# Weighing steps, output weights, gates and staged loads in a two-part attention kernel

## The chip, the cores and the metric

The kernel runs on one core of one Trainium2 chip. The metric is the time that the device needs for one execution, in microseconds (us); the kernel before is given by the median of three runs. The span in a profile is the time from the first to the last recorded event of one further execution, which the profiler recorded; that execution's own time is given beside its span.

The engines of the core are named as the profile names them: PE (TensorE, matrix products; PEld its weight loads), DVE (VectorE), ACT (ScalarE), POOL (GpSimd) and SP (SyncE, which here only issues DMAs). SPq and ACTq are DMA issues by SP and ACT.

## The reference

Two independent attentions over 2048 positions with model width 576 and 32 heads of width 18. Each ends in its own output projection, and the two outputs are put side by side. All of it is float32.

```
# A: one key head and one value head shared by 32 query heads, no mask
q = (x @ wq) in 32 heads;  k = x @ wk;  v = x @ wv          # k, v: 2048 x 18
p = softmax(q @ k.T * 18**-0.5)
outA = (p @ v) @ wo

# B: 32 heads, 4 segments of 512 positions, a memory M, z carried over the segments
phi = lambda t: where(t > 0, t + 1, exp(t))
g = sigmoid(beta)                                            # one number per head
M, z = 0, 0
for s in range(4):
    p = softmax(qs @ ks.T * 18**-0.5 + causal_mask)          # inside the segment
    a_dot = p @ vs
    a_mem = (phi(qs) @ M) / (phi(qs) @ z + 1e-6)
    o[s] = g * a_mem + (1 - g) * a_dot
    M, z = M + phi(ks).T @ vs, z + sum(phi(ks))
outB = o @ wo
```

## The kernel before

**First phase, 0 to about 330 us.** The projections of A and B are computed, each as a sum of products of split parts, and stored to DRAM scratch: `qA`, `kA`, `qB`, `kB`, `vB`. In the first 21 us the weights of A come in five pieces. ScalarE casts each to `wAh` (L196), VectorE takes the rest to `wAl` (L197), and TensorE begins to project (L208). In program order the gates come behind the first of A's four chunks of positions: `gt` becomes the sigmoid of beta, and `omg` is 1 minus it. Both are 128 x 5 tiles; column t holds the values of head tile t, one row per head and head dimension. The five loads of a column each (L267) are issued on ScalarE's DMA queue, with `gt`'s exponential (L270) on ScalarE and three small instructions on VectorE behind them. Further on, the memory's numerators `numB` (with the factor g in them) and denominators `denB` of segments 1 to 3 are computed and stored to scratch.

**Second phase, about 330 us to the end.** Attention runs in *turns*. A turn takes three score items. One item is two heads by 512 queries by 128 keys of A, or by one of three groups of keys of a segment of B. TensorE computes the scores into `E` (L765 for A, L774 for B). ScalarE exponentiates (L783), for one item of three from a copy `W` that VectorE made (L780). One of the 32 items of a block of A is exponentiated on VectorE by a polynomial instead (L738 to L748, with the tiles `PD` and `q`), one step a turn. For B, GpSimd then sets the masked half of the diagonal squares of `P` to zero (`affine_select`, L788). Two turns later TensorE multiplies `P` with the values into `O` (L813). VectorE copies `O` out, and SP stores it to scratch, `oA` or `oB` (L825). Row 0 of each head there is the sum of the softmax.

A *block* is four heads of one chunk (A) or of one segment (B): 32 blocks of A with 11 turns each, and 32 blocks of B with 2 turns each. The blocks of B are put in pairs behind blocks of A by the list `after`. Below, "segment 1, first pair" is the pair of blocks of B with heads 0 to 7 of segment 1. Every pair of blocks needs a stack of queries and keys (`stA`, `stB`), which `prefetch` loads ahead of its use, and every segment of B its values `vseg`.

**From the sums to the output projection.** The heads of a chunk or segment make five *head tiles*: t = 0 to 3 with 7 heads (126 rows), t = 4 with 4 heads (72 rows). Once the block with heads 24 to 27 is done (t = 0 to 3 follow from it), and again once the last block is done (t = 4), `finish` enters a chain of steps in a list `later`; `due` runs from it, once a turn, what has come up to its turn:

1. `begin`, one turn later: `sums` loads the softmax sums, and for segments 1 to 3 the denominators, into `sm`.
2. `inv`, `d1` turns later: `inverses` takes the reciprocal on VectorE (L618) and stores it to `rA`, `rB` and `rdB` in scratch (L620, L622).
3. `load`, as room is found: `load_heads` loads the head tile `o` (L632), the inverses spread over the rows, `rb` (L633), and for segments 1 to 3 also `numB` and the inverse denominators `rb2`.
4. `heads`, `d2` turns later: one GpSimd instruction per step, at most two in a turn. `weigh` gives them: for A the product with `rb` (L644); for B first the product with `omg` (L647, `part`), then that with `rb`; for segments 1 to 3 also the product of `nb` with `rb2`, and the addition.
5. When all five tiles are weighed, the output projection of that chunk or segment, `out_proj`, goes into `fill` one turn later. `run_fill` runs one step of four matrix products (L662) in a turn, 60 steps in all. It uses the weights `woA` and `woB`, which `load_wo` loads (L595) by five DMAs each.

What is left in `fill` after the last turn is run out, and then comes the projection of A's last chunk.

**What sets the order.** The instructions of PE, ACT and DVE are issued in the order written (`manual_schedule`). GpSimd's and SP's queues are not in that list: the scheduler orders them when the kernel is built, so a step that the program asks for in a later turn may stand earlier in those two queues.

Of the kernel before, what the change touches and what calls it, by code (L numbers as in the profile page):

```python
# [68 lines left out]
def attention_pair_kernel(ctx, tc, a_xT, a_w, a_wo, b_xT, b_w, b_wo, b_beta, ident_d, hmask_d, bmask_d, cmask_d, sel_d, zmask_d, selx_d, sely_d, out):  # L69
# [30 lines left out]
    gt = cp.tile([128, 5], F32, name="gt")  # L100
    omg = cp.tile([128, 5], F32, name="omg")
# [43 lines left out]
    with ExitStack() as ph:  # L145
# [75 lines left out]
        for c in range(NCH):  # L221
# [34 lines left out]
            if c == 0:  # L256
# [8 lines left out]
                for t in range(5):  # L265
                    lo, nh = H0[t], HT[t]
                    nc.scalar.dma_start(  # L267
                        gt[: RT[t], t : t + 1], b_beta[lo : lo + nh][:, None].to_broadcast([nh, DH])[:, :, None]
                    )
# [345 lines left out]
    def inverses(ab, c, lo, hi, said):  # L615
        sm, R, w, mem = said
        n = 2 if mem else 1
        nc.vector.reciprocal(sm[:R, :n], sm[:R, :n])  # L618
        r_d = rA if ab == "A" else rB
# [4 lines left out]
    def load_heads(ab, c, t):  # L624
        o_d, r_d = (oA, rA) if ab == "A" else (oB, rB)
        if (ab, c) not in parts:
            parts[ab, c] = pa.tile([128, 5, C], F32, name="o", bufs=2)
        tiles = [parts[ab, c][:, t], pa.tile([128, C], F32, name="rb", bufs=4)]
        if ab == "B" and c > 0:
            tiles += [pa.tile([128, C], F32, name=n, bufs=3) for n in ("nb", "rb2")]  # L630
        lo, n, R = H0[t], HT[t], RT[t]
        nc.sync.dma_start(tiles[0][:R], o_d[c][lo : lo + n, 1:VW, :])  # L632
        nc.sync.dma_start(tiles[1][:R], r_d[c][lo : lo + n, None, :].to_broadcast([n, DH, C]))  # L633
        if ab == "B" and c > 0:
            nc.sync.dma_start(tiles[2][:R], numB[c][DH * lo : DH * lo + R])
            nc.sync.dma_start(tiles[3][:R], rdB[c][lo : lo + n, None, :].to_broadcast([n, DH, C]))
        return tiles

    def weigh(ab, c, t, tiles):

        R = RT[t]
        o, rb = (x[:R] for x in tiles[:2])
        v = nc.gpsimd
        own = lambda: v.tensor_tensor(o, o, rb, op=ALU.mult)  # L644
        if ab == "A":
            return [own]
        part = lambda: v.tensor_scalar(o, o, omg[:R, t : t + 1], None, op0=ALU.mult)  # L647
        if len(tiles) == 2:
            return [part, own]
        nb, rb2 = (x[:R] for x in tiles[2:])  # L650
        return [
            part,
            own,
            lambda: v.tensor_tensor(nb, nb, rb2, op=ALU.mult),
            lambda: v.tensor_tensor(o, o, nb, op=ALU.add),
        ]
# [193 lines left out]

    def at(k, cost, ready, step):
# [3 lines left out]
    def due(k, most=2, heavy=2):  # L855

        cost = 0
        for e in [e for e in later if e[0] <= k]:
# [7 lines left out]
    def finish(k, ab, c, hg):  # L866
# [3 lines left out]
        box = {}  # L870
# [19 lines left out]
        def load(k, t):  # L890
            loaded[0] += 1
            box[t, t] = load_heads(ab, c, t)
            at(k + d2, 1, lambda: True, lambda k, t=t: heads(k, t))

        def heads(k, t):
            if not isinstance(box[t, t][0], type(heads)):
                box[t, t] = weigh(ab, c, t, box[t, t])
# [4 lines left out]
            loaded[0] -= 1  # L902
# [13 lines left out]
    with tc.manual_schedule(engines={ENG.PE, ENG.Activation, ENG.DVE}):  # L916
# [3 lines left out]
        turns, prods = [], []  # L920
# [6 lines left out]
        for k in range(len(turns) + 2):  # L927
# [108 lines left out]
```

## Time and profile before

| | before |
|---|---|
| median of 3 runs | 1471.53 us (1470.94 to 1474.15) |
| profiled execution, own time | 1476.41 us |
| its span | 1474.7 us |
| mean granted TensorE clock | 0.988 of full |
| ACT busy | 1194.1 us, 81% |
| DVE busy | 1030.4 us, 70% |
| POOL busy | 258.3 us, 18% |
| GpSimd masks (L788) | 192 instructions, 94.2 us |
| GpSimd products and sums of `weigh` (L644) | 40 instructions, 58.3 us |
| HBM traffic | 111 GB/s on average |

How to read the profile's lines: a row of the timeline has the start in us, the duration, the engine, the line, the operation, output<-inputs by the program's names, and the shapes; "x3" says how many neighbours were put together, and the brackets how long the engine had been idle before, and on what it waited. A row of a table of windows has the stretch, then the engine's busy time in it (with the number of instructions) for each engine asked for, the granted TensorE clock, the busy share of the DMA engines, and the DMA rate in GB/s. A row of waits has the waiting line and its releaser, the time in all, the number of waits, and the longest.

### The profile page before, as it was taken

To read this page: it belongs to the slowest core of one execution; us is meant where nothing else is said; L and a number is where in the kernel's file an instruction comes from. 1 tells how busy PE (TensorE), PEld (TensorE's weight loads), DVE (VectorE), ACT (ScalarE), POOL (GpSimd) and SP (SyncE) were. 2 spreads that over 40 slices of the span, in tenths; PEclk is the share of its full clock that TensorE was granted. 3 is DMA by queue.
4 is the path that set the end of the run, shared out by engine and by line. 5 is a ranking of instruction groups with operands and counts; after the bars stand their busy time and mean duration, and the time that the engine had idled before them with its cause. 6 is when DMAs were issued, how large, how long until landed. Compare 5 with 4: busy or idle time off the path is not lost.

```text
span 1474.7 us, 40733 instructions
## 1 busy us (share of the span) xinstructions
PE 1435.0 (97%) x17540; PEld 844.3 (57%) x17540; DVE 1030.4 (70%) x1209; ACT 1194.1 (81%) x1424; POOL 258.3 (18%) x311
## 2 busy tenths in 40 slices
PE   8889999999998999999999999999999999999998
PEld 5658878764454455555555555555555555555555
DVE  6474754646775577787777797777778887787761
ACT  3343334339998899999999999999999999999960
POOL 1031000001134112712110270031113500010001
PEclk9999999999999999999999999999999999999999
DMA  6775643445456154534222342233113221110022
GB/s 194 233 235 186 194 155 110 157 153 166 130 147 186 50 162 143 155 105 131 84 71 56 121 152 63 79 110 106 44 37 103 85 72 32 56 55 17 9 87 79
DMA packets 87986, 166.31 MB, mean 113 GB/s; under 512 B 12480, under 2 KB 21242, under 8 KB 87626
## 3 DMA queue, kind: packets, MB, share of 16 engines
q1 hardware_dynamic: 81510, 157.82, 34.2%
q10 hardware_dynamic: 6291, 5.85, 1.3%
q8 instruction: 138, 2.26, 0.6%
q14 instruction: 47, 0.38, 0.1%
HBM read 96.15 MB, written 67.49 MB: 111 GB/s over the span
## 4 chain that ended last, share of the span: by engine, by line
PE 60%; ACT 10%; issue 3%; DMA 2%; DVE 1%; SPq 1%; POOL 0%; ACTq 0%; DVEq 0%; POOLq 0%
PE O L813 28%; PE E L765 17%; PE F L662 11%; ACT P L783 10%; PE E L774 3%; PE E L662 1%; DMA oB<-oe 1%; DVE W L780 1%; PE O L662 1%; DMA rb<-rB 1%; DMA sm<-oA 0%; DMA rB<-sm 0%; SPq L595 0%; POOL o L644 0%; DVE q L742 0%
## 5 line engine op out<-in xcount | busy, mean ns | idle before, releaser
L783 ACT ACTIVATE P<-E 128x1024 f32<-128x1024 f32 (+1 forms) x800 | 788.4, 1077 | 23.2 <-PE E L765 11.4
L780 DVE COPY W<-E 128x1024 f32<-128x1024 f32 (+1 forms) x384 | 460.9, 1200 | 196.4 <-PE E L765 127.5
L813 PE MATMUL O<-P,VA 128*32 128x256 f32 x7936 | 511.4, 381 | 0.0
L783 ACT ACTIVATE P<-W 128x1024 f32<-128x1024 f32 (+1 forms) x384 | 433.9, 1130 | 2.0 <-DVE W L780 1.2
L813 PEld LDWEIGHTS O<-P,VA 128*32 128x32 f32 x7936 | 263.0, 110 | 148.1 <-issue 11.8
L765 PE MATMUL E<-stA,kstA 56*128 56x512 f32 x1920 | 331.4, 440 | 3.1 <-ACT P L783 1.5
L765 PEld LDWEIGHTS E<-stA,kstA 56*128 56x128 f32 x1920 | 155.0, 184 | 182.0 <-ACT P L783 121.3
L788 POOL TENSOR_SCALAR_AFFINE_SELECT P<-P 128x256 f32<-128x256 f32 (+1 forms) x192 | 94.2, 493 | 461.4 <-ACT P L783 427.5
L662 PE MATMUL F<-woB,o 126*32 126x192 f32 (+1 forms) x1920 | 127.8, 339 | 3.0 <-POOL o L644 3.0
L745 DVE SCALAR_TENSOR_TENSOR q<-q,PD 128x1024 f32<-128x1024 f32 x96 | 122.1, 1272 | 0.0
L644 POOL TENSOR_TENSOR o<-o,rb 126x512 f32<-126x512 f32 (+1 forms) x40 | 58.3, 1460 | 322.6 <-DMA o<-oA 143.2
L813 PE MATMUL O<-P,vseg 128*32 128x256 f32 (+2 forms) x1536 | 83.9, 349 | 4.0 <-POOL P L788 4.0
L110 ACT CAST qp<-pj 126x512 fp32r<-126x512 f32 (+1 forms) x56 | 32.6, 584 | 66.1 <-DVE kmB L360 49.8
L662 PEld LDWEIGHTS F<-woB,o 126*32 126x32 f32 (+1 forms) x1920 | 38.5, 108 | 72.7 <-issue 58.4
L662 PE MATMUL F<-woA,o 126*32 126x192 f32 (+1 forms) x1240 | 77.6, 338 | 1.7 <-DVE osb L687 1.7
L111 DVE TENSOR_TENSOR qp<-pj,qp 126x512 fp32r<-126x512 f32 (+1 forms) x56 | 38.3, 686 | 55.6 <-ACT qp L110 55.4
L208 PE MATMUL pj<-xh,wBh 128*126 128x512 f32 x180 | 73.7, 413 | 2.8 <-DVE xh L180 2.8
L822 DVE COPY oe<-O 128x512 f32<-128x512 f32 x64 | 44.3, 692 | 42.0 <-PE O L813 41.4
L208 PE MATMUL pj<-xh,wBl 128*126 128x512 f32 x180 | 72.2, 401 | 0.0
L813 PEld LDWEIGHTS O<-P,vseg 128*32 128x32 f32 x1536 | 48.4, 110 | 31.0 <-POOL P L788 5.5
L774 PE MATMUL E<-stB 56*128 56x256 f32 (+3 forms) x512 | 63.1, 354 | 2.4 <-ACT P L783 1.9
L208 PE MATMUL pj<-xl,wBh 128*126 128x512 f32 x144 | 59.8, 415 | 0.0
(134 smaller groups left out, 1400.1 us busy)
## 6 DMA issues: line engine op xcount, KB each, us to landing
stB<-kB SPq DMA_DIRECT2D x96, 144.0 KB
stB<-qB SPq DMA_DIRECT2D x32, 288.0 KB
stA<-qA SPq DMA_DIRECT2D x30, 288.0 KB
oA<-oe SPq DMA_DIRECT2D x32, 256.0 KB
oB<-oe SPq DMA_DIRECT2D x32, 256.0 KB
qA<-qp SPq DMA_DIRECT2D x16, 504.0 KB
kB<-qp SPq DMA_DIRECT2D x16, 504.0 KB
qB<-qp SPq DMA_DIRECT2D x16, 504.0 KB
```

Source lines behind the costliest of these rows:

```text
L111: nc.vector.tensor_tensor(qp[:R, 1, :n], src, qp[:R, 0, :n].bitcast(F32), op=ALU.subtract)
L208: nc.tensor.matmul(dst, w[:, c0 : c0 + M], x, start=i == 0, stop=i == len(ops) - 1)
L644: own = lambda: v.tensor_tensor(o, o, rb, op=ALU.mult)
L662: nc.tensor.matmul(dst[32 * j : 32 * j + 32], parts[ab, c][: RT[t], t, r0 : r0 + 32], wo[ab][: RT[t], t, c0 : c0 + n], start=start, stop=stop,
L745: steps.append(lambda a=a: v.scalar_tensor_tensor(q, q, a, p, op0=ALU.add, op1=ALU.mult))
L765: nc.tensor.matmul(e[:, j], kstA[rows, 128 * kt : 128 * kt + 128], st[rows, h, :], start=True, stop=True)
L774: nc.tensor.matmul(e[:, j, c0 : c0 + 512 - 128 * k], st[rows, 4 + h, ks], st[rows, h, 128 * k :], start=True, stop=True)
L780: nc.vector.tensor_copy(src[:, :, :n], e[:, :, :n])
L783: nc.scalar.activation(p[:, :, :n], src[:, :, :n], AF.Exp, scale=SCALE)
L788: nc.gpsimd.affine_select(diag, diag, pattern=[[0, 2], [0, m], [1, 128]], base=0, channel_multiplier=-1, compare_op=ALU.is_ge, fill=0.0)
L813: nc.tensor.matmul(o[32 * j : 32 * j + 32, q0 : q0 + n], v, p[:, j % 2, p0 : p0 + n], start=m == hf == 0, stop=last and hf == 1,)
L822: nc.vector.tensor_copy(osb, o)
```

## The change

- *Turns.* `due` lets no weighing step on GpSimd run in a turn when that turn or one of the two after it has score items of B (`near`).
- *Output weights.* `load_wo` is called in blocks 0 and 1 of A's first chunk, in place of blocks 2 and 5.
- *Gate.* `gt` and `omg` get two more columns, which hold the gate in the layout of the sums (4 rows a head for 28 heads; 32 rows a head for 4 heads), with two more loads on ScalarE's queue. `inverses` multiplies B's inverse sums by 1 - g on VectorE, and the `part` step (L647) is gone from `weigh`. All of `weigh` on GpSimd is then one instruction for A and for segment 0, and three for segments 1 to 3.
- *Stages.* `load` is split. `load_heads` loads `o` alone, right behind the inverses; `load_inverses` loads the rest `d2` turns later, when there is room in one pool of ten tiles, which takes the place of the pools of four, three and three. `heads` follows `d3` turns after that.
- *Delays.* Behind a block come: the sums after 2 turns (1 before), the inverses after 5 (4 or 5 before), the inverses' loads after 3 more, and the first weighing after 6 more (6 or 8 from the inverses before). For the last chunk: 0, 2, 0 and 3 (0, 2 and 3 before). `fill` gets the projection two turns after the last weighing (one before).

```diff
-    gt = cp.tile([128, 5], F32, name="gt")
-    omg = cp.tile([128, 5], F32, name="omg")
+    gt = cp.tile([128, 7], F32, name="gt")
+    omg = cp.tile([128, 7], F32, name="omg")
...
+                for t, lo, hi, n in ((5, 0, 28, 4), (6, 28, 32, 32)):
+                    nc.scalar.dma_start(
+                        gt[: n * (hi - lo), t : t + 1], b_beta[lo:hi][:, None].to_broadcast([hi - lo, n])[:, :, None]
+                    )
...
         nc.vector.reciprocal(sm[:R, :n], sm[:R, :n])
+        if ab == "B":
+            g = 5 if lo == 0 else 6
+            nc.vector.tensor_scalar(sm[:R, 0], sm[:R, 0], omg[:R, g : g + 1], None, op0=ALU.mult)
...
     def load_heads(ab, c, t):
...
+        nc.sync.dma_start(parts[ab, c][: RT[t], t], (oA if ab == "A" else oB)[c][H0[t] : H0[t] + HT[t], 1:VW, :])
+
+    def load_inverses(ab, c, t):
+        lo, n, R = H0[t], HT[t], RT[t]
+        tiles = [pa.tile([128, C], F32, name="rb", bufs=10)]
+        r_d = rA if ab == "A" else rB
+        nc.sync.dma_start(tiles[0][:R], r_d[c][lo : lo + n, None, :].to_broadcast([n, DH, C]))
         if ab == "B" and c > 0:
+            tiles += [pa.tile([128, C], F32, name="rb", bufs=10) for _ in range(2)]
+            nc.sync.dma_start(tiles[1][:R], numB[c][DH * lo : DH * lo + R])
+            nc.sync.dma_start(tiles[2][:R], rdB[c][lo : lo + n, None, :].to_broadcast([n, DH, C]))
         return tiles
...
-        own = lambda: v.tensor_tensor(o, o, rb, op=ALU.mult)
-        if ab == "A":
-            return [own]
-        part = lambda: v.tensor_scalar(o, o, omg[:R, t : t + 1], None, op0=ALU.mult)
-        if len(tiles) == 2:
-            return [part, own]
...
+        steps = [lambda: v.tensor_tensor(o, o, rb, op=ALU.mult)]
+        if mem:
+            nb, rb2 = mem
+            steps += [
+                lambda: v.tensor_tensor(nb, nb, rb2, op=ALU.mult),
+                lambda: v.tensor_tensor(o, o, nb, op=ALU.add),
+            ]
+        return steps
...
     def due(k, most=2, heavy=2):
         cost = 0
+        near = [its[n][0] for t in turns[k : k + 3] for n, pr in t]
+        heavy *= "B" not in near
...
-        d1, d2 = (2, 3) if last else (4, 6) if (ab, c) == ("B", 0) else (5, 8)
+        d0, d1, d2, d3 = (0, 2, 0, 3) if last else (2, 5, 3, 6)
...
             for t in ts:
-                at(k, 0, room, lambda k, t=t: load(k, t))
+                at(k, 0, place, lambda k, t=t: load(k, t))
+
+        def place():
+            return (ab, c) in parts or len(parts) - filled[0] // FILL < 2
+
+        def load(k, t):
+            load_heads(ab, c, t)
+            at(k + d2, 0, room, lambda k: weights(k, t))
...
         def room():
-            return loaded[0] < (3 if ab == "B" and c > 0 else 4) and ((ab, c) in parts or len(parts) - filled[0] // FILL < 2)
+            return loaded[0] + need <= 10
+
+        def weights(k, t):
+            loaded[0] += need
+            tiles = load_inverses(ab, c, t)
+            box[t, t] = weigh(ab, c, t, tiles)
+            at(k + d3, 1, lambda: True, lambda k: heads(k, t))
...
-                at(k + 1, 0, lambda: True, lambda k: fill.append(out_proj(ab, c)))
+                at(k + 2, 0, lambda: True, lambda k: fill.append(out_proj(ab, c)))
-        at(k + (0 if last else 1), 0, lambda: hg not in summing, begin)
+        at(k + d0, 0, lambda: hg not in summing, begin)
...
-                    if it in (("A", 0, 2, 4), ("A", 0, 5, 4)):
-                        load_wo(*(("B", b_wo) if it[2] == 2 else ("A", a_wo)))
+                    if it in (("A", 0, 0, 8), ("A", 0, 1, 8)):
+                        load_wo(*(("B", b_wo) if it[2] == 0 else ("A", a_wo)))
```

More of the change, by code (lines that the diff above doesn't have):

```diff
@@ L637, in load_heads @@
         return tiles
     def weigh(ab, c, t, tiles):
-        R = RT[t]
-        o, rb = (x[:R] for x in tiles[:2])
+        o, (rb, *mem) = parts[ab, c][: RT[t], t], [x[: RT[t]] for x in tiles]
         v = nc.gpsimd
-        own = lambda: v.tensor_tensor(o, o, rb, op=ALU.mult)
-        if ab == "A":
-            return [own]
-        part = lambda: v.tensor_scalar(o, o, omg[:R, t : t + 1], None, op0=ALU.mult)
-        if len(tiles) == 2:
-            return [part, own]
-        nb, rb2 = (x[:R] for x in tiles[2:])
@@ L651, in weigh @@
[L651 to L656, printed above, removed]
+        steps = [lambda: v.tensor_tensor(o, o, rb, op=ALU.mult)]
[6 more added lines that the diff above has]
+        return steps
     def out_part(ab, c, i, t, dst, c0, n, start, stop):
@@ L849, in attention_pair_kernel @@
     later, weighed, loaded, summing = [], {}, [0], set()
+    turns, prods = [], []
     def at(k, cost, ready, step):
@@ L869, in finish @@
         lo, hi = (0, 28) if hg == 6 else (28, 32)
-        box = {}
+        box, need = {}, 3 if ab == "B" and c > 0 else 1
         weighed.setdefault((ab, c), 0)
         last = (ab, c) == blocks[-1][:2]
-        d1, d2 = (2, 3) if last else (4, 6) if (ab, c) == ("B", 0) else (5, 8)
+        d0, d1, d2, d3 = (0, 2, 0, 3) if last else (2, 5, 3, 6)
         def begin(k):
```

18 lines of the change are left out of this document (1 added, 17 removed).

## The prediction, made before the changed kernel ran

> **What bounds the kernel now.** I read the page first, then ScalarE's exponentials in stretches, then the timelines of the engines in the stretches that fell out of step, and the waits last.
>
> ```profile
> span 1474.7 us, 40733 instructions
> ...
> PE 1435.0 (97%) x17540; PEld 844.3 (57%) x17540; DVE 1030.4 (70%) x1209; ACT 1194.1 (81%) x1424; POOL 258.3 (18%) x311
> ```
>
> The attention part begins near 330 us. There ScalarE's exponentials set the pace. The next view gives the exponentials alone (their busy time, the granted TensorE clock, DMA) in five stretches that I chose: a pair of score blocks of B without output projection (4.66 us), two pairs that went wrong, a pair with projection steps beside it, and a block of A (29.14 us).
>
> ```profile
> core 0: us, ACT busy (x), PEclk, DMA share, GB/s
> 406.91:411.57 4.66, 4.66 (x8) 1.00 0.00 0
> 459.00:470.28 11.28, 5.28 (x8) 0.73 0.47 143
> 499.49:510.14 10.65, 5.29 (x7) 0.68 0.01 2
> 553.49:558.31 4.82, 4.82 (x8) 1.00 0.01 3
> 728.04:757.18 29.14, 28.62 (x32) 1.00 0.39 114
> ```
>
> In the good pairs ScalarE is busy all the time, in a block of A 28.62 of 29.14 us. So work taken off GpSimd, VectorE or the DMA queues gives nothing there. Only stretches two and three lose time: 11.28 - 4.66 = 6.62 us and 10.65 - 4.82 = 5.83 us. The timelines of ScalarE and TensorE say what they waited for (in brackets, idle time before and its releaser):
>
> ```profile
> 466.73 1.56 ACT L783 ACTIVATE P<-E 128x768 f32<-128x768 f32 x2 [4.77 <-POOL P L788]
> ...
> 506.60 1.62 ACT L783 ACTIVATE P<-E 128x768 f32<-128x768 f32 x2 [4.28 <-PE E L774]
> ...
> 463.49 1.32 PE L813 MATMUL O<-P,vseg 128*32 128x256 f32 x16 [3.31 <-POOL P L788]
> ...
> 502.51 0.86 PE L662 MATMUL F<-woB,o 72*32 72x192 f32 x8 [2.97 <-POOL o L644]
> ```
>
> In the first, TensorE's products of B wait for GpSimd's causal mask (L788). In the second, a projection step waits for GpSimd to weigh B's last heads (L644, 72 rows); the next scores stand behind it in TensorE's queue. GpSimd's timeline shows why both are late:
>
> ```profile
> 451.26 4.65 POOL L647 TENSOR_SCALAR o<-o,omg 126x512 f32<-126x512 f32 x3 [21.48 <-DMA o<-oB]
> 455.88 1.29 POOL L644 TENSOR_TENSOR o<-o,rb 126x512 f32<-126x512 f32 x1
> 457.85 1.28 POOL L644 TENSOR_TENSOR o<-o,rb 126x512 f32<-126x512 f32 x1 [0.69 <-DMA rb<-rB]
> 459.09 0.41 POOL L788 TENSOR_SCALAR_AFFINE_SELECT P<-P 128x256 f32<-128x256 f32 x1
> 459.87 1.26 POOL L644 TENSOR_TENSOR o<-o,rb 126x512 f32<-126x512 f32 x1 [0.37 <-DMA rb<-rB]
> ...
> 500.81 0.42 POOL L788 TENSOR_SCALAR_AFFINE_SELECT P<-P 128x256 f32<-128x256 f32 x1 [23.72 <-ACT P L783]
> 501.20 1.26 POOL L644 TENSOR_TENSOR o<-o,rb 72x512 f32<-72x512 f32 x1
> ```
>
> The weighing waits for its loads, and the masks wait behind it; the 72-row multiplication of 501.20 stands in the queue behind a mask of the next pair, for no need of its own.
>
> **The change, part by part.** *The second stall.* In the built program GpSimd's queue is another one. The last two multiplications of B's segment 0 now stand behind the masks of the first two score blocks of segment 1 and ahead of those of the third, so they run from about 465 us, when those masks are done, and have until 499 us. Nothing else is late there: the projection takes this tile in the turn that begins at 499.49. I take the 5.83 us as gone; what keeps this from being certain is only that the load of its inverses comes later in SP's queue, behind a whole stack of B, and it has over 25 us to spare.
>
> *The first stall.* It is not removed by the rule on turns alone. The queue still has three multiplications (rows as that of 455.88) ahead of the first mask of segment 1, though the program asks for them five turns later: the order of GpSimd and SP is not the one written out by hand. So the question is when the third inverse tile lands. SP's queue before:
>
> ```profile
> 441.31 3.20 SPq L595 DMA_DIRECT2D woB<-b_wo  x5
> 444.56 0.35 SPq L620 DMA_DIRECT2D rB<-sm  x1
> 444.96 2.33 SPq L632 DMA_DIRECT2D o<-oB  x3
> 449.82 2.27 SPq L633 DMA_DIRECT2D rb<-rB  x3
> ...
> 440.00:445.00 5.00, 4.66 (x56) 2.39 (x58) 4.27 (x5) 5.00 (x6) 0.00 (x0) 1.00 0.78 260
> ...
> 455.00:460.00 5.00, 4.61 (x64) 2.34 (x53) 3.27 (x4) 5.00 (x8) 3.95 (x5) 1.00 0.69 199
> ...
> woB<-b_wo SPq DMA_DIRECT2D x4, 283.5 KB
> ```
>
> The two windows end with the DMA rate, 260 and 199 GB/s: the load is limited by transfer. The change takes woB, some 1.3 MB (five of up to 283.5 KB), out of this place. It puts the reads of all five head tiles and a part of the next B stack ahead of the inverses, where three were: two tiles and that part, about 0.7 MB. The inverses are computed two turns later, but their store met a queue that was blocked until 444.56 and now meets one that is busy with the head tiles until about the same time. So the net is 0.6 MB less in front, 2.7 us at 220 GB/s (between the two windows). The third tile, which GpSimd took at 459.87, then comes near 457.2. Its multiplication (1.26) and three masks (0.41 each) end near 459.7; TensorE asked for them near 460 (463.49 less 3.31). I leave 0.7 us of the stall: gain 5.9. Bounds: all 6.62, if the tiles come at 456 or sooner; and if they come no earlier than before, 459.87 + 1.26 + 1.23 = 462.4 against 460, a wait of 2.4, priced at 6.62/5.5 of lost time per us waited (460 to 465.5 was the wait before) 2.9, a gain of 3.7.
>
> *Twenty multiplications of GpSimd gone, eight small ones of VectorE new.* GpSimd's 4.65 us above are three of the twenty; they were paid in the stalls already. Elsewhere GpSimd is hidden, but it slows VectorE:
>
> ```profile
> 659.48 1.29 POOL L644 TENSOR_TENSOR o<-o,rb 126x512 f32<-126x512 f32 x1 [2.10 <-DMA rb<-rA]
> ...
> 659.52 2.33 DVE L742 SCALAR_TENSOR_TENSOR q<-PD 128x1024 f32<-128x1024 f32 x1
> ...
> ACT P L783 <- DVE W L780: 1.2, 3, 0.5
> ```
>
> ScalarE waited 1.2 us in all for VectorE's copies. With 20 of 90 weighings gone I take 0.3 of it; bounds, +1.2 gained and 1.2 lost if other collisions fall worse. The eight new VectorE instructions are small and lie in its idle 30%; ScalarE waits for VectorE only those 1.2 us. I put 0.2 lost on them and on the two projection steps below.
>
> *The tail.* The projection of each block now starts 2 turns earlier from the second on, so two more of its steps run in turns and two fewer behind the last turn. Before, a reciprocal stood in VectorE's queue ahead of copies that free TensorE's banks:
>
> ```profile
> 1437.27 0.25 DVE L618 RECIPROCAL sm<-sm 128x16 f32<-128x16 f32 x1 [3.46 <-DMA sm<-oA]
> ...
> 1437.79 1.83 PE L662 MATMUL F<-woA,o 126*32 126x192 f32 x40 [1.14 <-DVE osb L687]
> 1439.44 1.81 PE L662 MATMUL O<-woA,o 126*32 126x192 f32 x40
> ```
>
> It now comes a turn later, two copies further on, some 3 us, and the sums that it waits for landed at 1437.2: the 1.14 us go. Five steps take 1439.44 - 1437.79 = 1.65 us, two steps 0.66. Gain 1.8, bounds 0.7 and 1.8.
>
> *The start.* Two more loads of four-byte values go into ScalarE's queue between the weight casts of the first projection:
>
> ```profile
> 11.62 0.68 ACTq L267 DMA_DIRECT2D gt<-b_beta  x1
> 12.34 0.71 ACT L196 CAST wAh<-wr 128x618 fp32r<-128x618 f32 x1 [4.38 <-DMA gt<-b_beta]
> ...
> 17.02 0.21 ACT L270 ACTIVATE gt<-gt 128x5 f32<-128x5 f32 x1 [3.08 <-DMA gt<-b_beta]
> 18.25 0.71 ACT L196 CAST wAh<-wr 128x618 fp32r<-128x618 f32 x1 [1.03 <-DMA wr<-a_w]
> ...
> 18.99 0.81 DVE L197 TENSOR_TENSOR wAl<-wr,wAh 128x618 fp32r<-128x618 f32 x1 [1.13 <-ACT wAh L196]
> ...
> 21.00 0.46 PE L208 MATMUL pj<-xh,wAh 128*114 128x512 f32 x1 [0.95 <-DVE xh L184]
> ```
>
> The last of five was issued until 12.30 and its value was there at 17.0: 4.7 us. The seventh is issued behind the fourth cast: 12.34 + 0.71 + 0.7 + 0.71 + 0.7 = 15.2, there at 19.9. Gate (0.2), then the fifth cast at 20.1 instead of 18.25: 1.8 us later, and VectorE, which also does the gate first, and TensorE with it. If the loads come quicker it costs nothing (the cast waits for its own weights until 18.25). TensorE waits for inputs that come by DMA several times later on, which can take some of it up; I take 1.0, bounds 0 and 1.8.
>
> [...] In the stall of 459 to 470 the granted clock was 0.73 of full on average, against 1.00 in the stretches beside it. [...]
>
> Both output-weight loads move into the first 60 us of attention: ScalarE there waits for nothing, and the stack that each is put ahead of is used more than 20 us later. I cost them at nothing; were that cover gone, each is 3.2 us of SP's queue.
>
> **The sum.** -5.9 - 5.8 - 0.3 + 0.2 - 1.8 + 1.0 = -12.6 us. Of the profiled execution (1476.41 us, its span 1474.7 and 1.7 around it) 1463.8 is left. That execution stands 4.9 us above the median of the runs, 1471.53; the sum from the median gives 1458.9.
>
> **Rivals.** (1) The change does not do what it says: the three weighings ahead of the masks still wait as long as before. For it: the queue's order, and that the inverses are computed two turns later. Against it: woB is gone from in front. The bound above (2.9 of the first stall stays) gives 1461; were all of it to stay, 6.6, it is 1465. Chance 0.18. (2) The start costs more. The clock in the first stall was 0.73 over 11.28 us, 3.0 us of clock lost; were the longer gap at 21 us followed by the same, the start costs 1.8 + 3.0 and the sum gives 1462.7. It decides if TensorE's gap there exceeds 3.3 us, the idle time of 463.49. [...] Chance 0.07. (3) Slower: a new stall at the first masks of segment 2. There the 72-row weighing of A's first block has moved in GpSimd's queue from behind four masks to behind one, while its inverses are computed a turn later.
>
> ```profile
> 674.32 0.36 SPq L620 DMA_DIRECT2D rA<-sm  x1
> ...
> 683.72 1.28 POOL L644 TENSOR_TENSOR o<-o,rb 72x512 f32<-72x512 f32 x1
> ```
>
> The store of 674.32 moves to about 677.1 (a turn is 29.14/10.7 = 2.7 us), its load to 679 and its landing to about 682; TensorE asks for those masks near 685. It costs from a landing past 683 on, 1.2 us per us. To outweigh 12.6 it must land past 693, 14 us after its issue; the store and load of 444.56 and 449.82 together took 15 us until 459.87 in the busiest stretch, so it is not excluded. The time it would then give is 1474 or more. Chance 0.04; a small part of it, one or two us, is in the range.
>
> **Numbers.** My forecast, 1458.9, has 0.68, rivals 0.18, 0.07 and 0.04; 0.03 is for a gain that comes back as other waits so that nothing is left. The low end takes all of the first stall (-0.7), no cost of the start (-1.0) and the most of the ports (-0.9), and a first stall whose following turns also recover: 1455. The high end takes the first stall whole (+5.9) and a start at 1.8: 1466. What the measurement can tell is about 0.2%, 2.9 us: faster 0.93, same 0.03, slower 0.04.
>
> **What would show it.** Right: no ScalarE wait over 1 us between 455 and 515 us; the pairs at 459 and 499 last 4.7 to 5.5 us at clock 1.00; the fifth weight cast at 19 to 20 us; no VectorE wait for the last reciprocal's sums. The first step is wrong if TensorE's products still wait over 2 us for L788's successor near 460; the whole is wrong if a wait of several us shows at the first masks of segments 2 or 3, or in the first 60 us of attention.

## The result, and the profile after

The changed kernel takes 1465.59 us (median of 9 runs, 1464.75 to 1468.93), against 1471.53 us (1469.82 to 1474.15) for the kernel before: a ratio of 0.9964, with a 95% interval of 0.9953 to 0.9974. That is a gain of 5.9 us where 12.6 were forecast. The sign was right, and so was the cause of both stalls. The size was not, and most of the miss is the start, which the forecast put at 1.0 us and which costs 5.

The profiled execution took 1467.1 us. The top of its page, and ScalarE's exponentials in the two stretches of two turns that had gone wrong:

```profile
span 1465.4 us, 40738 instructions
...
PE 1429.3 (98%) x17540; PEld 843.1 (58%) x17540; DVE 1033.6 (71%) x1217; ACT 1193.1 (81%) x1424; POOL 224.7 (15%) x291
```

```profile
core 0: us, ACT busy (x), PEclk, DMA share, GB/s
462.92:469.01 6.09, 5.08 (x7) 1.00 0.50 149
497.73:502.57 4.84, 4.84 (x8) 1.00 0.01 3
```

The two turns that had lasted 10.65 us last 4.84 at full clock: the second stall is gone. Those that had lasted 11.28 last 6.09. GpSimd's and TensorE's timelines there:

```profile
459.28 1.28 POOL L654 TENSOR_TENSOR o<-o,rb 126x512 f32<-126x512 f32 x1 [25.57 <-DMA rb<-rB]
460.84 1.29 POOL L654 TENSOR_TENSOR o<-o,rb 126x512 f32<-126x512 f32 x1 [0.28 <-DMA rb<-rB]
462.57 1.27 POOL L654 TENSOR_TENSOR o<-o,rb 126x512 f32<-126x512 f32 x1 [0.44 <-DMA rb<-rB]
463.80 4.39 POOL L793 TENSOR_SCALAR_AFFINE_SELECT P<-P 128x256 f32<-128x256 f32 x10
...
464.27 2.14 PE L818 MATMUL O<-P,vseg 128*32 128x256 f32 x24 [1.20 <-POOL P L793]
...
474.74 3.38 POOL L654 TENSOR_TENSOR o<-o,rb 126x512 f32<-126x512 f32 x2 [4.92 <-DMA rb<-rB]
```

Three multiplications still stand ahead of the masks, as forecast. TensorE waits 1.20 us for the masks, where it had waited 3.31. The other two run at 474.74, behind the masks.

The start, by ScalarE's and TensorE's timelines:

```profile
12.34 0.83 ACTq L272 DMA_DIRECT2D gt<-b_beta  x1
13.35 0.71 ACT L197 CAST wAh<-wr 128x618 fp32r<-128x618 f32 x1 [0.31 <-DMA wr<-a_w]
13.49 0.58 ACTq L272 DMA_DIRECT2D gt<-b_beta  x1
20.21 0.21 ACT L275 ACTIVATE gt<-gt 128x7 f32<-128x7 f32 x1 [6.15 <-DMA xr<-a_xT]
21.42 0.71 ACT L197 CAST wAh<-wr 128x618 fp32r<-128x618 f32 x1 [1.01 <-DMA wr<-a_w]
...
24.17 0.46 PE L209 MATMUL pj<-xh,wAh 128*114 128x512 f32 x1 [4.12 <-DVE xh L185]
```

The fifth cast comes at 21.42 us, not at 18.25. TensorE pauses 4.12 us, not 0.95. (The releaser in the brackets of 20.21 is the last to come by the profile; the exponential reads `gt` alone. The brackets of 21.42 are as they say: that cast waited for its weights, `wr`. More on this below.)

TensorE also stands longer ahead of the first scores of attention, before and after:

```profile
329.32 1.17 PE L765 MATMUL E<-st,kstA 56*128 56x512 f32 x6 [1.35 <-SPq L500]
...
333.49 1.16 PE L770 MATMUL E<-st,kstA 56*128 56x512 f32 x6 [2.51 <-SPq L505]
```

Since the forecast was made from one execution, both kernels were profiled again, unchanged: three more executions of before and two more of after. The table gives the mean length of each stretch, between starts of ScalarE's exponentials.

| stretch | before, 4 executions | after, 3 | forecast | measured |
|---|---|---|---|---|
| up to the first exponential | 329.8 (328.2 to 331.6) | 334.8 (333.8 to 336.6) | +1.0 | +5.0 |
| from there to segment 1 | 123.8 | 124.1 | 0 | +0.3 |
| first pair of segment 1 and the turn after | 17.8 (17.2 to 18.5) | 11.9 (11.4 to 12.8) | -5.9 | -5.9 |
| second pair of segment 1 and the turn before | 16.6 (16.2 to 17.6) | 11.5 (11.5 to 11.6) | -5.8 | -5.1 |
| from there to the last turn | 908.4 | 909.1 | -0.1 | +0.7 |
| from the last turn to the end | 50.6 | 49.3 | -1.8 | -1.3 |
| span | 1471.8 | 1465.6 | -12.6 | -6.2 |

(Between the two pairs lie 24.8 us in all of them.)

### The profile page after: what moved, and what is told of

Same layout as the page of the kernel before. It is cut to its first block, busy times and chain, and to the rows that moved or that the text cites. A ratio compares the mean times of both kernels' runs of the same rounds, so it can differ in the third digit from the quotient of the medians.

```text
span 1465.4 us, 40738 instructions
## 1 busy us (share of the span) xinstructions
PE 1429.3 (98%) x17540; PEld 843.1 (58%) x17540; DVE 1033.6 (71%) x1217; ACT 1193.1 (81%) x1424; POOL 224.7 (15%) x291
## 4 chain that ended last, share of the span: by engine, by line
PE 63%; ACT 8%; DMA 3%; issue 2%; DVE 1%; POOL 0%; SPq 0%; DVEq 0%; POOLq 0%; ACTq 0%
PE O L818 29%; PE E L770 18%; PE F L667 11%; ACT P L788 8%; PE E L779 3%; PE E L667 1%; PE O L667 1%; DMA sm<-oB 1%; DMA stA<-qA 0%; DMA rB<-sm 0%; DMA stB<-kB 0%; DVE W L785 0%; DMA stB<-qB 0%; DMA out<-osb 0%; DMA rb<-rB 0%
```

## The experiments

Ratios are to the kernel before, with 95% intervals. The changed kernel stands at 0.9964 (0.9953 to 0.9974).

**The start: the two extra loads alone.** The kernel before, with the lines

```diff
+                for t, lo, hi, n in ((5, 0, 28, 4), (6, 28, 32, 32)):
+                    nc.scalar.dma_start(gt[: n * (hi - lo), t : t + 1], ...)
```

> The kernel before with the two extra loads of the gate and seven columns in gt and omg, and nothing else; the two new columns are not used. Theory 1 (the loads alone cost the start): slower than the kernel before by 3.8 us, about 1475.3, with a TensorE pause of about 4.1 us near 21 us. Rival (the start's lateness is waited out later where TensorE waits for transfers anyway, or is chance): within 1 us of 1471.5.

It took 1478.34 us, 1.0053 (1.0037 to 1.0070). TensorE's timeline in it:

```profile
24.98 0.46 PE L208 MATMUL pj<-xh,wAh 128*114 128x512 f32 x1 [3.92 <-DVE xh L184]
```

The loads alone bring back the pause and cost at least as much as theory 1 said. Attention begins at 334.8 us; nothing later took any of the delay up.

**The start: the extra loads on another queue.** In the changed kernel, the two columns in a tile of their own:

```diff
-                    nc.scalar.dma_start(gt[: n * (hi - lo), t : t + 1], ...)
+            if c == 1:
+                    nc.gpsimd.dma_start(g2[: n * (hi - lo), t : t + 1], ...)
+            if c == 3:
+                nc.scalar.activation(g2, g2, AF.Exp, scale=-1.0)   # and three on VectorE
```

> The changed kernel, with the two extra columns of the gate in a tile of their own: their loads go to GpSimd's DMA queue behind the second chunk of A, their exponential and three VectorE instructions behind the fourth. ScalarE's queue at the start is then that of the kernel before. Theory 1 (the two extra loads between the weight casts make the start late): TensorE's pause at 21 us is 0.95 us again instead of 4.12, the clock stays up, and the time is 3.8 us below the changed kernel's 1465.6, about 1461.8, ratio to the kernel before 0.993 to 0.994. Rival (the 3.8 us by which attention begins later is a difference between two single executions): attention begins at 333 to 335 us again and the time is 1465 to 1466, ratio 0.996.

1463.84 us, 0.9944 (0.9929 to 0.9959); attention began at 331.3. ScalarE's and TensorE's timelines:

```profile
13.87 0.20 ACT L281 ACTIVATE g<-g 128x2 f32<-128x2 f32 x1
14.04 0.71 ACT L197 CAST wAh<-wr 128x618 fp32r<-128x618 f32 x1
17.21 0.21 ACT L271 ACTIVATE gt<-gt 128x5 f32<-128x5 f32 x1 [2.47 <-DMA gt<-b_beta]
18.58 0.71 ACT L197 CAST wAh<-wr 128x618 fp32r<-128x618 f32 x1 [1.16 <-DMA wr<-a_w]
...
21.33 0.46 PE L209 MATMUL pj<-xh,wAh 128*114 128x512 f32 x1 [0.34 <-DVE xh L185]
```

The pause is gone, as theory 1 has it, but not because the exponential is later: the first phase isn't ordered by hand (that begins with attention), and the scheduler put the new one at 13.87. What helped is that GpSimd had issued the two loads by 3.3 us, ahead of most of the weights: they had landed by 8.7 us, and the fifth weight by 18.50. (The queue and the time of issue changed together here; this run can't tell them apart.) By the medians this is 1.8 us below the changed kernel, where 3.8 were expected. The expected ratio lies in the interval, but so does a part of the changed kernel's, so the gain in time is not clear of noise here; the start is.

**The start: only the exponential later.** The changed kernel with `if c == 1:` ahead of the gate's exponential and its three VectorE instructions.

> The changed kernel with all seven gate loads where they are, but the gate's exponential and its three VectorE instructions behind the second chunk of A instead of the first. Theory 1a (what makes the start late is that ScalarE and VectorE wait for the landing of the last load): TensorE's pause at 21 us is at most 1 us and the time about 3.9 us below the changed kernel, near 1461.7, ratio 0.992 to 0.994. Rival 1b (issuing two more loads from ScalarE between the casts is itself what delays them): the pause is over 2 us and the time within 2 us of 1465.6.

1467.32 us, 0.9969 (0.9959 to 0.9978). As an experiment this told nothing on 1a or 1b: the scheduler moved the exponential back to its old place, at 19.93 us ahead of the fifth cast, with a pause of 3.83 us behind it. Its trace does speak against 1a, as that of the changed kernel does: the fifth weight landed in several pieces, whose times the trace records, the last one at 21.02 us, and the cast began at 21.10. Without the exponential it could not have begun sooner. An edit to program order doesn't move an instruction here unless the built order shows it.

**The start: all seven loads on GpSimd's queue** (and the split inverses, below). In program order the loads stand behind the second chunk, the exponential behind the fourth.

> As the run with the split inverses and the extra loads on GpSimd's queue, but with all seven gate loads on GpSimd's queue, so that ScalarE issues none. Theory 1d (the five old loads, 4.1 us of issues ahead of ScalarE's third cast, cost the kernel before 1 us of its start too, the pause of 0.95 us at 21 us): that pause is gone, attention begins 1 us earlier, ratio 0.001 below that run's. Rival (the projection of the first chunk is bound by TensorE and by the loads of its inputs): same time within 0.5 us; or, if seven loads on GpSimd's queue land late, the exponential waits ahead of the casts and the start is later.

1468.56 us, 0.9979 (0.9968 to 0.9991): near the second rival, but not for its reason. The scheduler put the gate's exponential ahead of the third cast, and its values came at 16.6 us:

```profile
16.62 0.21 ACT L277 ACTIVATE gt<-gt 128x7 f32<-128x7 f32 x1 [8.34 <-DMA gt<-b_beta]
18.20 1.48 ACT L197 CAST wAh<-wr 128x618 fp32r<-128x618 f32 x2 [1.38 <-DMA wr<-a_w]
...
13.95 2.02 PE L209 MATMUL pj<-xh,wAh 128*114 128x512 f32 x4 [4.86 <-DVE xh L181]
```

The third cast did not wait for the exponential, but for the third weight: by the trace's landings that weight was there at 18.18 us, and at 12.04 in the kernel before. The inputs `xr`, on which VectorE's casts wait, were late, too (TensorE's pause of 4.86 us). So GpSimd's queue was not quicker here. With two loads there the third weight came 1.2 us later than in the kernel before and the fifth 0.3 (13.24 and 18.50 in the run with two loads on GpSimd's queue, 12.04 and 18.17 before); with seven the third came 6.1 later.

**The gate's part undone.** The changed kernel with the old five columns, no product with the gate in `inverses`, and `part` back in `weigh`.

> The changed kernel with the gate's part undone: five columns and five loads, no product with the gate on VectorE, the multiplication by 1 - g (L647 of the kernel before) back on GpSimd ahead of each weighing of B. Theory 1 and the forecast of the contention: the start is 3.9 us earlier, the first stall longer by up to 2 us (three multiplications of 1.55 us more ahead of the masks, which can run while their inverses are on the way), turns 94, 198 and 302 keep 0.2 of their 0.5 us less; 2 to 3 us below the changed kernel, about 1463. Rival (the multiplications that went were worth more than the start cost): 1466 or more.

1462.84 us, 0.9936 (0.9922 to 0.9950), as theory 1 said: the change is faster without this part of it. Attention begins at 329.0 us. Of the twenty GpSimd multiplications that come back, those ahead of the masks of segment 1 ran before their inverses had landed, and TensorE waited 0.67 us for the masks:

```profile
446.89 5.61 POOL L647 TENSOR_SCALAR o<-o,omg 126x512 f32<-126x512 f32 x3 [0.50 <-DMA o<-oB]
452.73 1.29 POOL L648 TENSOR_TENSOR o<-o,rb 126x512 f32<-126x512 f32 x1 [0.23 <-DMA rb<-rB]
...
458.44 2.14 PE L812 MATMUL O<-P,vseg 128*32 128x256 f32 x24 [0.67 <-POOL P L787]
```

Of the turns named, 94 still lasts 3.27 us, 198 and 302 last 2.9.

**The rule on turns.** The changed kernel without `heavy *= "B" not in near`.

> The changed kernel without the rule on turns (the line with near is out of use), so that weighing steps are asked for in any turn. Theory 2 (the rule is what clears the second stall, as the change's words say): the pair of blocks near 499 us stalls again and the time is up to 5.8 us above the changed kernel, about 1471. Rival (GpSimd's queue is set by the scheduler, and the later steps for the sums, loads and weighings alone put the weighings behind the masks): no stall above 1 us there, time within 1 us of 1465.6.

1467.11 us, 0.9968 (0.9956 to 0.9980): the rival. There is no second stall, and GpSimd's order differs from that of the changed kernel in one place only, the 72-row multiplication of A's first chunk. The rule that the change names first does next to nothing. The second stall is also gone with the gate undone and with woB in its old place (next), so what is left to clear it is the later and split steps; these were not taken out one by one.

**The place of woB: undone, and alone.** The changed kernel with the old condition for `load_wo`; and the kernel before with the new one:

```diff
-                    if it in (("A", 0, 2, 4), ("A", 0, 5, 4)):
+                    if it in (("A", 0, 0, 8), ("A", 0, 1, 8)):
```

> The changed kernel with load_wo at its old places (blocks 2 and 5 of A's first chunk). Theory 4 (the load of woB ahead of the inverses made the first stall long): the third inverse tile of segment 0 lands several us later against the turns, TensorE waits over 3 us for the first masks of segment 1, and the time is 3 to 6 us above the changed kernel, 1468.5 to 1471.5. Rival (the steps behind the sums, and the weighing multiplications ahead of the masks, set the stall, and the transfers have room): the stall grows by less than 1.5 us, time 1465 to 1467.

> The kernel before with load_wo at its new places, and nothing else. GpSimd's queue then has all weighings of the first four head tiles of segment 0 ahead of the first mask of segment 1. Theory 4 (woB's transfer held back the inverses): their tiles land 3 to 5 us earlier, the first stall shrinks from 6 us to 2 to 3, the second stays at 4.5 to 5.8: gain 3 to 4 us, about 1468. Rival (the eight instructions ahead of the masks take up what the earlier landing gives): gain under 1.5 us.

Undone: 1472.3 us, 1.0001 (0.9990 to 1.0012). Alone: 1468.54 us, 0.9978 (0.9968 to 0.9988). TensorE's timelines, first undone, then alone:

```profile
467.92 3.32 PE L818 MATMUL O<-P,vseg 128*32 128x256 f32 x24 [3.88 <-POOL P L793]
```

```profile
459.06 2.14 PE L813 MATMUL O<-P,vseg 128*32 128x256 f32 x24 [0.84 <-POOL P L788]
...
497.48 0.87 PE L662 MATMUL F<-woB,o 72*32 72x192 f32 x8 [4.90 <-POOL o L644]
```

Theory 4 holds both ways. With woB in its old place the wait for the masks is 3.88 us, longer than before the change, although fewer multiplications stand ahead of them. With woB moved and nothing else, the wait is 0.84 us. The second stall stays then, and is longer (4.90 us waited, 2.97 before).

**Two steps for the inverses.** In the changed kernel VectorE's reciprocal of both sums, the gate and a step of the polynomial now meet in one turn. The timelines of VectorE and ScalarE in the changed kernel:

```profile
573.57 1.75 DVE L624 RECIPROCAL sm<-sm 112x256 f32<-112x256 f32 x1
575.35 0.29 DVE L627 TENSOR_SCALAR sm<-sm,omg 112x128 f32<-112x128 f32 x1
575.55 1.22 DVE L785 COPY W<-E 128x1024 f32<-128x1024 f32 x1
...
574.51 2.03 ACT L788 ACTIVATE P<-E 128x1024 f32<-128x1024 f32 x2
576.80 1.06 ACT L788 ACTIVATE P<-W 128x1024 f32<-128x1024 f32 x1 [0.27 <-DVE W L785]
577.77 1.92 ACT L788 ACTIVATE P<-E 128x1024 f32<-128x1024 f32 x2
```

This turn lasts from 574.51 to 577.77, 3.26 us instead of 2.76, and so do turns 198 and 302 (segments 2 and 3). The experiment is the run with the later exponential, without the rule on turns, and with

```diff
-        nc.vector.reciprocal(sm[:R, :n], sm[:R, :n])
+        nc.vector.reciprocal(sm[:R, 0], sm[:R, 0])      # sm[:R, 1] and its store one turn later
```

> The kernel of the run with the later gate exponential, also without the rule on turns, and with the inverses of segments 1 to 3 in two steps: the softmax sums and the gate in one turn, the memory's denominators in the next. In the changed kernel the reciprocal of 1.75 us and the gate's 0.29 us delayed VectorE's copy in three turns by 0.5 us each. Theory 5 (that queue on VectorE is what those turns lose): turns 94, 198 and 302 last 2.76 instead of 3.26 us, and the time is 1.5 us below that of the other kernel, near 1460.2. Rival (the second step collides with the next turn's copy instead): 0.5 us is lost in turns 95, 199 and 303, and the two times agree within 0.5 us.

1465.44 us, 0.9959 (0.9946 to 0.9972), 1.9 us below the run with the later exponential, whose start is built the same way, and level with the changed kernel; both intervals overlap this one, so the times alone show no gain. The turns do: the three last 2.76 us, and turns 95, 199 and 303 did not grow, as theory 5 has it. The reciprocal is two, of 0.94 us for 112x128:

```profile
577.43 0.94 DVE L624 RECIPROCAL sm<-sm 112x128 f32<-112x128 f32 x1
```

**Segment 0's inverses earlier**, on top of the split: `(1, 4, 0, 6) if (ab, c) == ("B", 0)`.

> The kernel with the split inverses, where segment 0 of B gets its sums after 1 turn (2), its inverses after 4 more (5) and the loads of the inverses without further delay (3). Theory 6 (what is left of the first stall comes from the late sums: the reciprocal of segment 0 was at 447.3 us in the changed kernel, 437.6 us before): the first pair of segment 1 shows no wait over 0.3 us, and the time is 1 us below the kernel with the split inverses, near 1459. Rival (the scheduler now puts weighing multiplications between the masks of segment 1, and they wait there for their inverses): a stall of 1 to 4 us at that pair, and 1 to 3 us slower than the kernel with the split inverses.

1469.56 us, 0.9988 (0.9978 to 0.9998): the rival. The scheduler put a multiplication behind a mask again, and the masks behind it waited for its inverses (GpSimd's timeline, then TensorE's):

```profile
461.51 0.43 POOL L796 TENSOR_SCALAR_AFFINE_SELECT P<-P 128x256 f32<-128x256 f32 x1
463.35 1.27 POOL L657 TENSOR_TENSOR o<-o,rb 72x512 f32<-72x512 f32 x1 [1.42 <-DMA rb<-rB]
464.57 3.93 POOL L796 TENSOR_SCALAR_AFFINE_SELECT P<-P 128x512 f32<-128x512 f32 x8
...
465.85 1.51 PE L821 MATMUL O<-P,vseg 128*32 128x256 f32 x16 [2.10 <-POOL P L796]
```

**More executions of the unchanged kernels.** The kernel before, three times more (the first beside the first experiments), and the changed kernel twice:

> The kernel before, unchanged, for a second profiled execution: the first was 1476.41 us, 4.9 us above the median of its runs. Theory 3 (the two stalls' length varies from execution to execution, and the first profile caught long ones): the two stalls together are shorter than 12.4 us by several us in this execution, and its time nearer to 1471.5. Rival (the stalls are the same every time and what varies lies elsewhere): both stalls within 0.5 us of 6.6 and 5.8 us, and the difference in time lies in other stretches.

> The kernel before, unchanged, a third profiled execution. In the first two, TensorE waited 3.31 and 3.29 us for the masks of segment 1 and 2.97 and 2.98 us for the weighing ahead of segment 1's third pair of heads, and yet the pairs lost 7.1 and 6.0, 5.8 and 4.5 us. Theory 7 (the waits are fixed by the order of work, what they cost is set by how long the clock stays down after them, which changes from execution to execution): waits of 2.7 to 3.4 and 2.9 to 3.0 us again; lost times between 5 and 7.5 and between 4 and 6 us; the lower the clock in the stretch, the greater the loss. Rival (the first profile was long because of something else, and the losses of 6.0 and 4.5 are what every other execution shows): losses within 0.3 us of these.

> The kernel before, unchanged, a fourth profiled execution: as the third.

> The changed kernel, unchanged, a second profiled execution. Theory 1 (the loads in ScalarE's queue): attention begins at 334 to 337 us, against 329 to 331 in the kernel before, with a TensorE pause near 24 us of 3.8 to 4.2 us. Theory 7: the first stall is 0 to 3.2 us, as it was in the kernels with the same order on GpSimd, and the second is gone. Rival: attention begins before 333 us, and the start was chance.

> The changed kernel, unchanged, a third profiled execution: as the second.

The new executions took 1472.54, 1474.39 and 1470.83 us, and 1466.49 and 1468.4 us. The waits were 3.29, 3.18 and 3.06 us for the masks, and 2.97 or 2.98 for the weighing, as in the first. The first three turns of the second pair, in the windows of the exponentials, for the first profile of before and then the fourth, with TensorE's wait in the fourth:

```profile
499.49:512.70 13.21, 7.85 (x10) 0.74 0.06 21
```

```profile
496.24:508.06 11.82, 7.62 (x11) 0.86 0.07 24
```

```profile
499.26 0.87 PE L662 MATMUL F<-woB,o 72*32 72x192 f32 x8 [2.98 <-POOL o L644]
```

For the same wait, 1.4 us more were lost where the clock averaged 0.74 instead of 0.86. The other two executions took 11.9 us at 0.86: theory 7 in its first half, and the rival on the size, since the first profile is the one that stands out. The mean hides two steps. In the first profile the clock was at 0.50 for 6.83 us from 501.7 on, in the fourth for 3.41 us from 498.7 on (TensorE alone; the first profile, then the fourth):

```profile
core 0: us, PE busy (x), PEclk, DMA share, GB/s
501.70:505.11 3.41, 2.60 (x28) 0.50 0.02 5
505.11:508.52 3.41, 3.41 (x34) 0.50 0.00 0
...
498.71:502.12 3.41, 2.86 (x32) 0.51 0.03 5
502.12:505.53 3.41, 3.41 (x55) 0.99 0.00 0
```

In the second of the two windows TensorE is busy throughout, but for 34 products instead of 55. The three turns of the first stall took 12.6 to 13.8 us, at clocks of 0.73 to 0.75 that don't follow them (0.50 for 6.83 us in each of the four); what sets that spread stays open. The changed kernel's start was late each time: attention began at 333.8 and 336.6 us, with pauses of 3.22 and 3.69 us, shorter than expected. What was left of the first stall in its first profile, 1.4 us, wasn't there in the other two.

**The best version.** The two extra loads on GpSimd's queue, and the split inverses.

> The run with the two extra gate loads on GpSimd's DMA queue, and the inverses of segments 1 to 3 in two steps; the rule on turns stays. In the run with the loads on GpSimd's queue the scheduler had put the new exponential at 13.9 us, ahead of the fourth weight cast, and still the start was that of the kernel before. Theory 1c (what cost the start is the queue that the two loads stood in, not the place of the exponential) and theory 5 (three turns lose 0.5 us to the long reciprocal): no TensorE pause over 1.5 us before 100 us, turns 94, 198 and 302 at 2.76 us, and the time 1.3 us below the run with the loads on GpSimd's queue, ratio to the kernel before 0.993 to 0.994. Rival (what that run gained was chance of the first 120 us): ratio 0.9955 to 0.997, as with the split alone.

1460.56 us (1458.97 to 1461.97, 5 runs), 0.9919 (0.9905 to 0.9934): faster than both kernels, 11.4 us below the 1472.00 of before beside it and 5.0 below the changed one's median. That is more than the 1.3 us expected over the run with the loads on GpSimd's queue; what the rest comes from no run shows. Attention begins at 328.2 us, the first stall is 0.4 us, turns 94, 198 and 302 last 2.76. ScalarE's waits over attention, where 5.0 us for scores of B, 4.8 for masks and 1.2 for copies had stood in the kernel before:

```profile
ACT P L1010 <- PE E L675: 40.8, 3, 39.7
ACT P L796 <- PE E L778: 10.3, 30, 0.6
```

What is left is the last projection and short waits for scores of A. The time is near what the prediction had promised of the change itself, but with a step that the change doesn't have.

## Why the prediction was right or wrong

**First stall: right in size, -5.9 forecast and -5.9 measured on average.** woB was what held the inverses back, and its move did what the sum said. Rival 1, that the weighings wait as long as before, did not come. That a version with earlier sums got slower shows how thin this is: it hangs on where the scheduler puts five multiplications.

**Second stall: right in cause, 0.7 us too large.** The weighing is behind the first pair's masks and long done. The 5.83 us came from an execution in which the clock stayed low for 6.83 us after the same wait, and not for 3.41. The three turns took 13.21 us in the one and 11.82 in the other; what kept the clock down for longer no run shows.

**Start: wrong, +1.0 forecast, +5.0 measured.** This is the step that decides the miss. Its working took the fifth cast's own weights as there by 18.25, whatever else was loaded, and priced only the wait for the gate: issued by 15.2, there at 19.9, the cast at 20.1. The gate came about then. The issue was over sooner, at 14.07, the value took 6.1 us instead of 4.7, and the seventh load landed at 20.1. What failed is the weights. Each half of the fifth weight lands in 16 pieces, by the trace's record of landings. In the kernel before, the last one was there at 18.17, 3.0 us behind the issue. In the changed kernel twelve were there by 19.12 and the last four only at 21.14 to 21.34, 1.0 us and more behind the seventh load. The fifth cast begins 0.08 us behind that last piece in both kernels (18.25 behind 18.17, 21.42 behind 21.34), with the two loads on GpSimd's queue (18.58 behind 18.50) and with the later exponential (21.10 behind 21.02): it waited for its weights and not for the exponential. That the small loads are what these pieces stood behind is read from the order of the landings, and from the runs that move the two loads alone or leave them out, where the last piece comes at 18.3 to 18.7 us.

Over the executions of both kernels the cast is 3.0 us later (21.16 against 18.20 on average). Another 0.8 us are lost by the end of the first phase. Then TensorE's wait ahead of the first scores, which stood in no term, grows by 1.6 us, to 2.51, 3.10 and 3.07 from 1.19 to 1.35; the first exponential follows 0.4 us sooner behind those scores. That wait is 2.46 to 3.40 us in every run with the two loads on ScalarE's queue, and at most 1.41 in the others; what lengthens it stays open. The discount to 1.0, because later pauses would take it up, had no row behind it.

The prediction's rival 2 gave this start 4.8 us, at a chance of 0.07, and is near the total by luck. Its condition, a pause over 3.3 us, held in two of the three executions (4.12 and 3.69, but 3.22). Its 1.8 for the cast measured 3.0, and against its 3.0 for the clock there is at most the 0.8. In the first 60 us the clock stood at 0.50 for 3.41 us in each execution of before, and for 6.83, 10.24 and 13.65 us after; in the rest of the first phase it stood so for longer in the kernel before (9.4 against 5.7 us on average), which gives part of it back.

**VectorE and the contention: -0.1 forecast, +0.7 measured.** Turns 94, 198 and 302 lose 0.5 us each, 1.5 in all. The prediction said that the new instructions lie in VectorE's idle 30%. But the inverses moved, too, and in the turns that they fall in now VectorE had no idle time. With the gate undone the first of the three turns still lost 0.5 us and the others 0.1, so the move and the gate's product both have a part. About half of the 1.5 comes back in other turns. That GpSimd no longer slows VectorE there would explain it, but was not followed turn by turn. In the kernel before, the polynomial's step on L742 took 1.21 to 1.22 us in all 27 turns without a GpSimd product beside it. Beside one it took 1.98 to 2.33 us in three of five turns (2.33 at 659.52); in the other two the product itself took 2.28 and 2.34 us, where that of 659.48 took 1.29. The forecast's low end lays this to ports; what causes it no run shows.

**Tail: -1.8 forecast, -1.3 measured.** The reciprocal no longer stands in the way, and the wait of 1.14 us is gone, as forecast. But the twelve groups of forty products that it stood among take 20.0 us instead of 20.9, so 0.2 of it came back between them; the rest of the 0.5 was not followed up.

**From one execution to the median.** The sum was made on an execution that was 4.9 us above its median, and was then taken off the median, as if all its terms were typical. Of about 6.3 us of miss in the table, 4.0 are the start, 0.3 the turns after it, 0.8 the stretch behind the stalls, 0.7 the second stall, and 0.5 the tail.

## What to carry to other kernels

When a change adds a load, ask which loads stand behind it, and not only when its own value will be there: here the gate's value came about when forecast, and the weights issued behind it came 2.4 to 3.2 us late. Read in the brackets what an instruction waits for before you decide that it waits for its neighbour. An engine's idle share says nothing on the turn in which a new instruction falls; look at what already stands in that turn. When a sum rests on stalls, take a second profile before you trust their size, and ask the built order, not the program, where a scheduler has put things: here one named rule did nothing, and one reordering was undone.

## What the runs showed of the hardware that was not expected

The cost of a wait was not its length here. Attention, whose pace ScalarE sets, lost 4.4 to 5.8 us for a TensorE wait of 2.97 or 2.98 us (11.82 and 13.21 us for three turns that take 7.40 in the changed kernel), with the clock at 0.74 to 0.86 behind them. These are averages: in the clock records of the first execution of each kernel the clock is 1.00 or 0.50, and the stays at 0.50, except the one cut off by the end of each trace, last 3.41 us (two before, four after) or 6.83 us (four before, one after). And the clock also fell where no pause was long. In the kernel with the gate undone, matmuls of the same shape go from 0.40 to 0.63 us at 26.77 us, and TensorE's pauses in the 6 us before were 0.46, 0.84 and 1.39 us, 2.69 in all (TensorE's timeline, then a window with its busy time and the clock, 0.50):

```profile
25.89 0.50 PE L209 MATMUL pj<-xh,wAh 128*126 128x512 f32 x1 [1.39 <-DVE qp L112]
26.23 0.40 PE L209 MATMUL pj<-xl,wAh 128*126 128x512 f32 x1
...
26.77 0.63 PE L209 MATMUL pj<-xh,wAh 128*126 128x512 f32 x1
...
26.77:29.80 3.03, 3.03 (x9) 0.50 0.84 284
```

What made the clock fall there no run shows.

A large load also came late behind small ones. The two extra loads carry 960 bytes, four at a time. The half of the fifth weight that decides the start carries 158 KB, and four of its 16 pieces landed 2.0 us behind the twelfth (19.12 to 21.14) where these loads had been issued ahead of it, and 0.1 us behind it (17.94 to 18.03) where they had not.
